# Opening of a fused GFNet and ELU-MLP kernel: x and a half-size table first, the filter straight into SBUF, a plain first unit, and the weights converted late

## The chip, the cores and the metric

The kernel runs on one core of a Trainium2 chip. The metric is the time of one execution in microseconds (us) on the device, as the median of several runs. A profile of one execution gives the rows that are read here. Its engines are TensorE (PE, with its weight loads as PEld), VectorE (DVE), ScalarE (ACT), GpSimd (POOL) and SyncE (SP), and 16 DMA engines that serve the queues of SP, ACT and POOL.

## The reference

```python
X = np.fft.rfft(x, axis=1)                       # x: (8, 3008, 256) float32
Y = X * (filt_r + 1j * filt_i)[None]             # filter: (1505, 256)
y = np.fft.irfft(Y, n=3008, axis=1)
h = y.reshape(24064, 256) @ w_in                 # w_in: (256, 2048) float64
g = np.where(h > 0, h, np.exp(np.minimum(h, 0)) - 1)
out = (g @ w_out).astype(np.float32)             # w_out: (2048, 256) float64
```

A Fourier filter runs along the sequence of each of the eight batches, and a two-layer perceptron with the ELU nonlinearity runs over all 24064 tokens. The weights come as float64, and the kernel works in float32.

## The kernel before

The transform of length 3008 is factored as 47 x 64 and done by matrix products with small tables. Rows of x are paired with their mirror rows: forward rows lie in the lower 64 partitions and mirrored rows in the upper 64. The stages of a batch are: a (the first factor, six units of four rows each), transposes, b (the second factor), the product with the filter on VectorE, bi and n (the inverse factors). The result y goes through a DRAM buffer (`yd`) between bi and n. The n units give tiles of y for the perceptron.

The perceptron is done in units (b, m), six per batch, and each unit in four quads q, one for each quarter of the 2048 hidden columns. One level of Strassen's scheme cuts the eight block products of a quad to seven, for the up projection (`up_steps`, line 607) and for the down projection (`down_steps`, line 692). For this the input needs four differences (`n_sums`, line 584), the weights need four sums (`w_sums`, line 839), and the up products are combined by additions on VectorE (line 630) and copies on ScalarE (line 633). ELU is Relu and Exp on ScalarE (lines 639 and 640) and a maximum on VectorE (line 644). The items (b, m, q) are numbered as quads 0 to 191, 24 to a batch. In the stream of quad i the up products of item i alternate with the down products of item i-1. The transform of batch b+1 is spread over the quads of batch b by a plan, `at(quad, place, fn)`, written by hand: places 2 and 3 lie after the third and fifth step of the first half of the quad, place 0 after that half, place 1 at the end. The order of the instructions on each engine is the order of the program (`manual_schedule`, line 878). Semaphores of DMAs issued by SP and ACT come from eight lanes used in turn, so such a DMA can have to wait for an earlier one of its lane; POOL's DMAs have eight lanes of their own.

The opening (lines 878 to 1007) does batch 0's transform by functions of its own, while nothing else is there to overlap:

- `x_load_first` (293) loads a unit of x in two DMAs, and its table `tf` in a third. `a_first` (303) does 16 matmuls a unit and copies the result to `zt` on ScalarE (315). `t_first` (318) transposes on TensorE.
- `f_arrange` (848) rearranges the filter in DRAM, from the inputs to the buffer `fd`, by DMAs of POOL; `f_read_first` (359) reads it into the tile `ff`. `f_pairs` (867) later rearranges `fd` into the order for the other batches.
- The loop over g from 0 to 9 runs `b_first` (381, with the four VectorE products of lines 376 to 379), `bi_first` (395) and `y_write_first` (407). `y_read` (524) then brings y back, and `n_unit(0, 0)` (line 545, `n_whole`) makes the first input tile.
- The weights are 16 pieces of 128 x 512 float64, two for w_in and two for w_out in each quarter. `w_fetch` (776) loads one as pairs of 32-bit words. `w_split` (801) takes the mantissa and the exponent by two bit operations on VectorE. `w_float` (807) makes floats of them by four operations on ScalarE (814). `w_join` (816) joins sign, mantissa and exponent on VectorE (820, 822, 829 or 835). `step(k)` is the split and float of piece k with the join of piece k-1. In the kernel before, pieces 0 to 6 are converted between the units of a, pieces 7 to 10 inside the g loop, 11 to 13 after it, and 14 and 15 in quads 0 to 2.

PSUM has four banks for general use, handed out in turn by `bank` (197), and four for the down products and the transposes.

Of the kernel before, what the change touches and what calls it, by code (L numbers as in the profile page):

```python
# [11 lines left out]
FP32 = mybir.dt.float32  # L12
# [29 lines left out]
def _make_tables():  # L42
# [27 lines left out]
    tf = np.ascontiguousarray(ta.reshape(P, H, 4, K2).transpose(0, 1, 3, 2)).reshape(P, H, P)  # L70
# [43 lines left out]
    lie = np.concatenate([2 * np.arange(24), 2 * np.arange(24) + 1])  # L114
    gb[:, :, lie] = gb[:, :, :48].copy()
    for t in (gr, gi):
        for o in (0, 64):
            t[o + lie] = t[o:o + 48].copy()
# [3 lines left out]
    tw = np.ascontiguousarray(tn[:, 0:8].reshape(4, K2, 8, 2, 2, 32).transpose(1, 0, 2, 4, 3, 5)).reshape(P, 8, P)  # L122
# [12 lines left out]
def kernel(  # L135
# [47 lines left out]
    edges = glob.tile([P, 2], FP32, name="edges")  # L183
    unit = glob.tile([P, P], FP32, name="unit")
    fd = fdp.tile([NG, 2, 48, 2, 2, D], FP32, name="fd")
# [107 lines left out]
    def x_load_first(c):  # L293
        t = xs[0, c]
        u = 1 if c == 0 else 0
        nc.sync.dma_start(t[HALVES[0]].rearrange("p u d -> p (u d)"), raw(x, XC * c, [[N1 * D, 64], [1, XC * D]]))
        nc.sync.dma_start(t[HALVES[1], u:XC, :], raw(x, N1 - XC * c - u, [[N1 * D, 64], [-D, XC - u], [1, D]]))
        if c < 2:
            nc.sync.dma_start(tas[0, c], tf_d[:, 4 * c:4 * c + 4, :])
        elif c % 2 == 0:  # L300
            nc.sync.dma_start(tas.pop(("pair", c // 2)), tf_d[:, 4 * c:4 * c + 8, :])
# [16 lines left out]
    def t_first(g):  # L318

        t = t2s[0, g] = t4p.tile([P, 4, D], FP32, tag="t4", name="tf") if g % 4 > 1 else t2[:, g % 4]  # L320
        for j in range(2):
            i = j + 2 * (g % 2 if g < 4 else 0)
            ps = psO.tile([P, 2, 256], FP32, tag="po%d" % i, name="po%d" % i)
            for u in range(2):
                k = 4 * g + 2 * j + u
                for dh in range(2):
                    nc.tensor.transpose(ps[0:ROWS, u, ts(dh, P)], zt[k // 16][dh][:, ts(k % 16, ROWS)], eye)  # L327
            nc.scalar.activation(out=t[0:ROWS, 2 * j:2 * j + 2, :], in_=ps[0:ROWS], func=AXT.Copy)
# [30 lines left out]
    def f_read_first(g, t):  # L359
        for a, r in enumerate((LO, HI)):  # L360
            nc.gpsimd.dma_start(t[r].rearrange("p c u d -> p (c u d)"), fd[g, a].rearrange("q c u d -> q (c u d)"))
# [12 lines left out]
    def products(re, im, f, sr, si, p, q):  # L374

        nc.vector.tensor_tensor(out=sr, in0=re, in1=f[:, 0], op=ALU.mult)
        nc.vector.tensor_tensor(out=si, in0=re, in1=f[:, 1], op=ALU.mult)
        nc.vector.scalar_tensor_tensor(out=p, in0=im, scalar=-1.0, in1=f[:, 1], op0=ALU.mult, op1=ALU.mult)
        nc.vector.tensor_tensor(out=q, in0=im, in1=f[:, 0], op=ALU.mult)
# [144 lines left out]
    def y_read(b, m, *parts):  # L524
        t = t4s[b, m] = t4p.tile([P, 4, D], FP32, tag="t4", name="t4")
        for k in parts or (slice(0, K2),):
            if whole(b, m):
                r = slice(4 * k.start, 4 * k.stop)
                nc.sync.dma_start(t[r], yds[b].rearrange("k (p i) d -> (k p) i d", p=4)[r, 4 * m:4 * m + 4, :])
                continue  # L530
            for r in range(2):
                o = 64 * r
                nc.sync.dma_start(t[o + 2 * k.start:o + 2 * k.stop].rearrange("q i d -> q (i d)"),
                                  yds[b][k.start + r:k.stop:2].rearrange("k (p i) d -> k p (i d)", p=4)
                                  [:, :, 4 * m * D:4 * m * D + 4 * D])
# [9 lines left out]
    def n_whole(b, m):  # L545
# [10 lines left out]
        b11, b12, b21, b22 = rows  # L556
        t = yp.tile([P, 2, 256], FP32, tag="yb", name="yb")[:, :, 0:h]
# [42 lines left out]

    COMBO = {1: 0, 2: 2, 3: 6, 4: 3, 5: 4, 6: 5, 7: 1}
# [5 lines left out]
    def up_steps(b, m, q):  # L607

        h = half(m)
# [82 lines left out]
    def down_steps(b, m, q):  # L692
        h = half(m)
# [82 lines left out]
    def w_fetch(k, queue=nc.gpsimd):  # L776
        q, j = divmod(k, 4)

        if k in (3, 4, 14, 15):
            wd = t2[:, k % 11 - 3].rearrange("p u d -> p (u d)")  # L780
        elif k == 10:
            wd = t1p.tile([P, XC, D], FP32, tag="t1", name="wd").rearrange("p u d -> p (u d)")
        elif k in (6, 7, 8, 9):
            wd = xp.tile([P, 2, 2, D], FP32, tag="xc", name="wd").rearrange("p k u d -> p (k u d)")
        else:
            wd = fbufs[{5: 0, 11: 0, 12: 1, 13: 2}.get(k, k)].rearrange("p c u d -> p (c u d)")
# [14 lines left out]
    def w_split(k):  # L801
        m, e, f, l = wts[k] = wtmp[{9: 2, 10: 1, 11: 0, 12: 3, 13: 4, 15: 5}.get(k, k % 2)]
# [4 lines left out]
    def w_float(k, *parts):  # L807
        m, e, f, l = wts[k]
        ef = e.bitcast(FP32)
        steps = ((l, wds[k][:, :, 0], AXT.Identity, 2.0 ** -52, 0.0), (f, m, AXT.Identity, 2.0 ** -20, 1.0),  # L810
                 (ef, e, AXT.Relu, -8.0, edges[:, 0:1]), (e, ef, AXT.Relu, -1.0, edges[:, 1:2]))
        for i in parts or range(4):
# [3 lines left out]
    def w_join(k, parts=(0, 1)):  # L816
        q, j = divmod(k, 4)
        m, e, f, l = wts[k]
        if 0 in parts:
            nc.vector.scalar_tensor_tensor(out=e, in0=wds.pop(k)[:, :, 1], scalar=0x80000000, in1=e,  # L820
                                           op0=ALU.bitwise_and, op1=ALU.bitwise_or)
            nc.vector.tensor_tensor(out=f, in0=f, in1=l, op=ALU.add)
        if 1 not in parts:
            return
        e = e.bitcast(FP32)
# [10 lines left out]
        if j % 2 == 1 and k < 7:  # L836
            w_sums(k)

    def w_sums(k, engine=nc.vector, parts=(0, 1, 2, 3)):
# [4 lines left out]
        for i in parts:  # L844
            o, x, y, op = sums[i]
            engine.tensor_tensor(out=o, in0=x, in1=y, op=op)

    def f_arrange():

        for c, src in enumerate((filt_r, filt_i)):  # L850
            for a in range(2):
                nc.gpsimd.dma_start(fd[:, a, 0:48:2, c, :, :].rearrange("g q u d -> q g (u d)"),
                                    raw(src, 2 * a, [[64 * D, 24], [4 * D, NG], [1, 2 * D]]))
                for u in range(2):
                    g0 = 1 if a == u == 0 else 0
                    for j, n in ((0, 16), (16, 7)):
                        nc.gpsimd.dma_start(fd[g0:NG, a, 1 + 2 * j:2 * (j + n):2, c, u, :].rearrange("g q d -> q g d"),
                                            raw(src, 64 * (j + 1) - 4 * g0 - 2 * a - u,
                                                [[64 * D, n], [-4 * D, NG - g0], [1, D]]))

                g0 = 0 if a else 1
                nc.gpsimd.dma_start(fd[g0:NG, a, 47, c, :, :].rearrange("g u d -> g (u d)"),
                                    raw(src, 4, [[2 * D, NG - g0], [1, 2 * D]]))
            nc.gpsimd.dma_start(fd[0, 0, 1:48:2, c, 0, :], raw(src, 32, [[64 * D, 24], [1, D]]))
            nc.gpsimd.dma_start(fd[0, 0, 47:48, c, 1, :], raw(src, 4, [[D, 1], [1, D]]))

    def f_pairs(c, u):

        src = fd.rearrange("g a q c u d -> (g a) q c u d")[:, :, c, u, :]
        dst = fp.rearrange("g (a u) k c h d -> (g a) u k c h d", u=2)[:, u, :, c, :, :]  # L870
        nc.sync.dma_start(dst[:, :, 0, :], src[:, 0:48:2, :])
        g = 1 - u
        nc.sync.dma_start(dst[g:, 1:24, 1, :], src[g:, 1:46:2, :])
        nc.sync.dma_start(dst[g:, 0, 1, :], nil_d[g:])
        if u == 0:
            nc.sync.dma_start(dst[0, :, 1, :], src[0, 1:48:2, :])

    with tc.manual_schedule():


        with tc.tile_pool(name="boot", bufs=1) as bp:
            ff = bp.tile([P, NG, 2, 2, D], FP32, name="ff")
# [9 lines left out]

            for z in zt[0] + zt[1]:
                nc.gpsimd.memset(z.rearrange("p (k r) -> p k r", r=ROWS)[:, :, 48:64], 0.0)
            for k in (1, 2, 3):
                w_fetch(k)
            f_arrange()
            w_fetch(0, nc.sync)
            for c in range(NXC):
                x_place_first(c)  # L900
            for c in range(3):
                x_load_first(c)
            w_fetch(4, nc.sync)
            nc.scalar.memzero(ff[:, 0:NG // 2])
            nc.vector.memset(ff[:, NG // 2:NG], 0.0)
            def places(m, e, c):
                wtmp.append((m.bitcast(U32), e.bitcast(U32), c[:, 0], c[:, 1]))

            def flat(t):
                return t.rearrange("p a b -> p (a b)")  # L910

            places(*(kp.tile([P, 512], FP32, tag=t, name=n) for t, n in (("k0", "wm"), ("k1", "we"))),
                   kp.tile([P, 2, 512], FP32, tag="c", name="wfl"))
            places(*(flat(sdp.tile([P, 2, D], FP32, tag="sd", name=n)) for n in ("wm", "we")),
                   t1p.tile([P, XC, D], FP32, tag="t1", name="wfl").rearrange("p (a b) d -> p a (b d)", a=2))
            for i, v in enumerate((1151.0 * 2 ** 23, 255.0 * 2 ** 23)):
                nc.vector.memset(edges[:, i:i + 1], v)
# [7 lines left out]
            for k in range(3):  # L925
                step(k)
            w_fetch(5, nc.sync)
            for c in (3, 4):
                x_load_first(c)
            a_first(0)  # L930
            w_fetch(6, nc.sync)
            x_load_first(5)
            nc.sync.dma_start(once, once_d)
            nc.sync.dma_start(gs, gs_d)
            step(3)
            for c in (1, 2):
                a_first(c)
                w_fetch(c + 6, nc.sync)
            step(4)
            a_first(3)  # L940
# [200 lines left out]
```

## Time and profile before

| what | value |
|---|---|
| time, median of 3 runs (lowest to highest) | 2551.03 us (2550.78 to 2551.74) |
| profiled execution: its time | 2553.3 us |
| profiled execution: span, first to last instruction | 2551.5 us |
| PE busy, share of the span | 2517.5 us, 99% |
| DVE busy | 2112.0 us, 83% |
| ACT busy | 1527.3 us, 60% |
| first matmul starts | 13.08 us |
| first product of `b_first` starts | 48.29 us |
| last product of the filter on VectorE ends | 75.15 us |
| first up product of quad 0 starts | 89.14 us |
| quad 6 starts | 164.46 us |

The first rows are read on the profile's page, the last five in its timeline. An engine's share counts matmuls, activations and vector operations; the issue of DMAs is not counted as busy. In the windows, the columns behind the length are busy us and number of instructions for PE, PEld, DVE, ACT and POOL, then the mean clock that TensorE was granted (1.00 is full), the mean busy share of the 16 DMA engines, and what they moved in GB/s. In the chain, a piece is work that the next piece waited for. A line of a matmul counts two records for one instruction of the program.

### The profile page before, as it was taken

The numbers are of one execution on the slowest core, as the hardware profiler recorded it, in microseconds if no ns is written. First come the engines' busy times: TensorE is split into PE (matmuls) and PEld (weight loads), VectorE is DVE, ScalarE is ACT, GpSimd is POOL, SyncE is SP. The second block draws the span as 40 slices with busy tenths as digits, with TensorE's granted clock in tenths as the row PEclk, the third lists the DMA queues.
The fourth block names the chain that finished last, engine by engine and source line by source line (L and its number), as shares of the span: only waits on it lengthen the run. The fifth ranks groups of instructions, "written<-read, shape, count | busy, mean of one in ns | idle before, by whom it ended". The sixth has DMA issues, their size and how long they took to land.

```text
span 2551.5 us, 45225 instructions
## 1 busy us (share of the span) xinstructions
PE 2517.5 (99%) x17266; PEld 2162.0 (85%) x17266; DVE 2112.0 (83%) x3649; ACT 1527.3 (60%) x2680; POOL 159.4 (6%) x315
## 2 busy tenths in 40 slices
PE   6999999999999999999999999999999999999999
PEld 5788889888898888988889888888889888898888
DVE  6878888888788888888888888788897888876766
ACT  6765556655565565565555656555555655555555
POOL 5001000010000000000000000000100010000000
PEclk9999999999999999999999999999999999999999
DMA  9662213422134231433215331243213322120010
GB/s 281 176 183 68 66 36 82 126 68 68 42 99 102 66 70 40 112 87 74 55 40 139 73 80 36 69 125 82 63 41 81 91 61 65 36 46 19 20 28 17
DMA packets 229452, 198.35 MB, mean 78 GB/s; under 512 B 128326, under 2 KB 201558, under 8 KB 229236
## 3 DMA queue, kind: packets, MB, share of 16 engines
q1 hardware_dynamic: 214740, 164.57, 26.2%
q0 software_dynamic: 14000, 30.44, 4.3%
q8 instruction: 136, 2.23, 0.4%
q14 instruction: 80, 0.66, 0.1%
q10 hardware_dynamic: 496, 0.46, 0.1%
HBM read 123.50 MB, written 78.12 MB: 79 GB/s over the span
## 4 chain that ended last, share of the span: by engine, by line
PE 97%; DMA 2%; DVE 1%; SPq 0%; issue 0%; ACT 0%; DVEq 0%
PE po L704 45%; PE phs L622 25%; PE phd L622 13%; PE pha L622 6%; PE psn L574 2%; PE pf L427 1%; PE pv L499 1%; DMA xc<-in_x_dram 1%; PE psa L246 1%; PE po L372 1%; DMA x<-in_x_dram 1%; PE po L327 0%; PE psr L372 0%; PE psa L265 0%; PE psa L308 0%
## 5 line engine op out<-in xcount | busy, mean ns | idle before, releaser
L704 PE MATMUL po<-g,wo 128*128 128x256 f32 (+1 forms) x5376 | 1317.6, 377 | 0.0
L704 PEld LDWEIGHTS po<-g,wo 128*128 128x128 f32 x5376 | 1010.7, 190 | 166.2 <-issue 52.4
L633 ACT ACTIVATE g<-phs 128x512 f32<-128x512 f32 (+1 forms) x576 | 338.8, 588 | 742.9 <-PE phs L622 741.5
L640 ACT ACTIVATE e<-e 128x512 f32<-128x512 f32 (+1 forms) x768 | 477.3, 621 | 24.4
L644 DVE SCALAR_TENSOR_TENSOR g<-e,g 128x512 f32<-128x512 f32 (+1 forms) x576 | 387.4, 673 | 13.6 <-ACT e L640 13.2
L630 DVE TENSOR_TENSOR g<-phd,g 128x512 f32<-128x512 f32 (+1 forms) x384 | 258.9, 674 | 158.1 <-ACT e L640 107.6
L622 PE MATMUL phs<-y,wi 128*128 128x256 f32 (+1 forms) x1536 | 387.6, 375 | 0.0
L622 PE MATMUL phd<-y,wi 128*128 128x256 f32 (+1 forms) x1504 | 380.3, 375 | 0.0
L639 ACT ACTIVATE e<-g 128x512 f32<-128x512 f32 (+1 forms) x576 | 354.4, 615 | 34.2 <-DVE g L630 26.7
L622 PEld LDWEIGHTS phs<-y,wi 128*128 128x128 f32 x1536 | 291.7, 190 | 33.3 <-ACT g L633 0.2
L622 PEld LDWEIGHTS phd<-y,wi 128*128 128x128 f32 x1504 | 284.8, 190 | 35.1 <-DVE g L630 2.7
L644 DVE SCALAR_TENSOR_TENSOR g<-e,phs 128x512 f32<-128x512 f32 (+1 forms) x192 | 129.9, 677 | 115.2 <-ACT e L640 115.2
L622 PE MATMUL phs<-yt,wi 128*128 128x256 f32 (+1 forms) x768 | 193.9, 375 | 0.9 <-ACT g L633 0.9
L622 PE MATMUL phs<-yb,wi 128*128 128x256 f32 (+1 forms) x768 | 193.8, 375 | 0.6 <-ACT g L633 0.6
L622 PE MATMUL pha<-yb,wi 128*128 128x256 f32 (+1 forms) x736 | 185.9, 375 | 0.0
L639 ACT ACTIVATE e<-phs 128x512 f32<-128x512 f32 (+1 forms) x192 | 112.3, 585 | 111.9 <-PE phs L622 111.8
L622 PEld LDWEIGHTS phs<-yt,wi 128*128 128x128 f32 x768 | 145.7, 190 | 17.9 <-ACT g L633 1.4
L622 PEld LDWEIGHTS phs<-yb,wi 128*128 128x128 f32 x768 | 143.9, 190 | 19.3 <-ACT g L633 1.0
L366 POOL DMA_DIRECT2D fall<-fp x224 | 110.1, 499 | 722.1 <-DVE r L472 697.1
L622 PEld LDWEIGHTS pha<-yb,wi 128*128 128x128 f32 x736 | 139.8, 190 | 16.1
L630 DVE TENSOR_TENSOR g<-pha,g 128x512 f32<-128x512 f32 (+1 forms) x192 | 129.3, 673 | 28.3 <-PE pha L622 28.3
L681 DVE TENSOR_TENSOR g<-g,g 128x512 f32<-128x512 f32 (+1 forms) x192 | 130.7, 681 | 6.7
(177 smaller groups left out, 2077.9 us busy)
## 6 DMA issues: line engine op xcount, KB each, us to landing
yd<-t SPq DMA_DIRECT2D x127, 192.0 KB
t<-yd SPq DMA_DIRECT2D x92, 256.0 KB
fall<-fp POOLq DMA_DIRECT2D x224, 96.0 KB, 2.9
t<-z SPq DMA_DIRECT2D x224, 96.0 KB
out_dram<-o SPq DMA_DIRECT2D x624, 32.0 KB
z<-t SPq DMA_DIRECT2D x144, 128.0 KB
xc<-in_x_dram SPq DMA_DIRECT2D x84, 128.0 KB
xc<-in_x_dram SPq DMA_DIRECT2D x161, 64.0 KB
```

Source lines behind the costliest of these rows:

```text
L246: nc.tensor.matmul(ps[k][1][a:a + 32, u, :], w[r, u, 32 * o:32 * o + 32], parts[o][r, u, :], start=True, stop=True, tile_position=(32 * k, a))
L366: nc.gpsimd.dma_start(t[32 * a:32 * a + 24].rearrange("p c u d -> p (c u d)"), fp[g, a].rearrange("q c u d -> q (c u d)"))
L372: nc.tensor.matmul(ps[:, u:u + w, :], table[k, v, :], r[k, u:u + w, :], start=n == 0, stop=n == len(rhs) - 1)
L574: nc.tensor.matmul(o, t[r, i - 4 * m, ds(dh * P + 64 * c, 64)], w[r, i - 4 * m, :], start=True, stop=True)
L622: nc.tensor.matmul(ps[:, a, 0:h], w_in[q][:, COMBO[n], a, :], y[n], start=start and a == 0, stop=True, skip_group_check=True)
L630: nc.vector.tensor_tensor(out=g[o], in0=i0, in1=i1, op=ALU.add)
L633: nc.scalar.activation(out=g[o], in_=i0, func=AXT.Copy)
L639: nc.scalar.activation(out=e, in_=src, func=AXT.Relu, scale=-1.0)
L640: nc.scalar.activation(out=e, in_=e, func=AXT.Exp, scale=-1.0)
L644: nc.vector.scalar_tensor_tensor(out=g[n], in0=es[n], scalar=1.0, in1=src, op0=ALU.subtract, op1=ALU.max)
L681: nc.vector.tensor_tensor(out=b12, in0=b22, in1=b12, op=ALU.subtract)
L704: nc.tensor.matmul(po[i][:, u, 0:h], w_out[q][:, COMBO[n], a, :], g[n][:, a, :], start=q == 0 and a == 0 and n in (1, 3, 6, 4), stop=True, ...
```

## The change

1. The table of the first factor is stored at half size (128 x 24 x 64) and loaded into the space of `t3f`. VectorE makes the full table of each unit from it (`a_table`: one copy and two multiplications by a sign). x is loaded first, ahead of everything but this table; then `once` and `gs`, two small constant tables.
2. The filter is loaded straight into `ff` by `f_first`, with forward rows and mirrored rows in separate ranges of partitions: forward rows on SP's queue ("f", 14 DMAs), the first 16 mirrored rows of a half on ACT's queue behind units 2, 3 and 5 of a ("m", 12 DMAs), the other 7 on POOL's queue ("s", 12 DMAs). `f_arrange`, `f_read_first` and `fd` are gone, and `f_pairs` reads the inputs, by one DMA more each.
3. All weights are fetched on SP behind the filter. `w_float` has three operations instead of four: the scaling of the mantissa has gone into the add of `w_join`, which is now a multiply-add. Pieces 0 and 1 are begun at the last two rounds of the g loop, 2 to 8 follow before `n_unit(0, 0)`, and 8 to 15 are finished in quads 0 to 3. All eight `w_sums` are done on VectorE in quads 3 to 6.
4. The first unit (0, 0) is done plainly, by eight block products (`plain_ups`, `plain_downs`), without `n_sums`, sums of weights and additions.
5. The writes of y go by POOL's queue (the last one's second half by ACT's), and the read of y for unit (0, 0) too. The units of x and a of batch 1, with their z writes, come one quad later (quads 3, 3, 4, 4, 5, 5 instead of 2, 2, 3, 3, 4, 4); `n_unit(0, 1)` is at place 0 of quad 2.

```diff
     def x_load_first(c):
...
-        if c < 2:
-            nc.sync.dma_start(tas[0, c], tf_d[:, 4 * c:4 * c + 4, :])
-        elif c % 2 == 0:
-            nc.sync.dma_start(tas.pop(("pair", c // 2)), tf_d[:, 4 * c:4 * c + 8, :])
+    def a_table(c):
+        t = th[:, XC * c:XC * c + XC]
+        o = tas[0, c].rearrange("p u (k f) -> p u k f", f=4)
+        nc.vector.tensor_copy(out=o[:, :, :, 0:4:2], in_=t)
+        for f, k in ((1, 1), (3, 0)):
+            nc.vector.tensor_scalar(out=o[:, :, :, f], in0=t[:, :, :, k], scalar1=signs, scalar2=None, op0=ALU.mult)
...
+    def f_first(k, n, parts, queue):
+        for c, src in enumerate((filt_r, filt_i)):
+            for a in range(2):
+                o, row, e = 64 * a, 16 * a + k, 1 if k == a == 0 else 0
+                if "f" in parts:
+                    queue.dma_start(ff[o:o + 24, c, k:k + n].rearrange("q k d -> q (k d)"),
+                                    raw(src, row, [[64 * D, 24], [1, n * D]]))
+                for j, m, part in ((0, 16, "m"), (16, 7, "s")):
+                    if part in parts:
+                        queue.dma_start(ff[o + 24 + j:o + 24 + j + m, c, k + e:k + n],
+                                        raw(src, 64 * (j + 1) - row - e, [[64 * D, m], [-D, n - e], [1, D]]))
+            if k == 0 and "f" in parts:
+                queue.dma_start(ff[24:48, c, 0], raw(src, 32, [[64 * D, 24], [1, D]]))
...
+    def plain_ups(b, m, q):
...
+        def step(i, j, k):
+            if k == 0:
+                held[i, j] = bank("php")
+            n, ps = held[i, j]
+            for a in range(2):
+                nc.tensor.matmul(ps[:, a, 0:h], w_in[q][:, 2 * k + i, a, :], rows[k][j],
+                                 start=k == a == 0, stop=True, skip_group_check=True)
+            if k == 1:
...
+                nc.scalar.activation(out=e, in_=src, func=AXT.Relu, scale=-1.0)
+                nc.scalar.activation(out=e, in_=e, func=AXT.Exp, scale=-1.0)
+                nc.vector.scalar_tensor_tensor(out=g[i, j], in0=e, scalar=1.0, in1=src, op0=ALU.subtract, op1=ALU.max)
...
     def w_join(k, parts="ab"):
...
+            w_sign(k)
+            nc.vector.scalar_tensor_tensor(out=f, in0=m, scalar=2.0 ** -20, in1=l, op0=ALU.mult, op1=ALU.add)
...
     with tc.manual_schedule():
...
+            nc.sync.dma_start(flat_th[:, 0:2 * XC], tf_d[:, 0:2 * XC])
+            for c in range(NXC):
+                x_load_first(c)
+                if c == 0:
+                    nc.sync.dma_start(flat_th[:, 2 * XC:H], tf_d[:, 2 * XC:H])
+            nc.sync.dma_start(once, once_d)
+            nc.sync.dma_start(gs, gs_d)
+            parts = ((0, 4), (4, 4), (8, 8))
...
+            for c in range(2):
+                a_table(c)
+            nc.vector.memset(ff[:, 1], 0.0)
+            for c in range(2, NXC):
+                a_table(c)
+            for c in range(NXC):
+                a_first(c)
+                if c == 0:
+                    for k, n in parts:
+                        f_first(k, n, "s", nc.gpsimd)
+                        f_first(k, n, "f", nc.sync)
+                if c in (2, 3, 5):
+                    f_first(*parts[c // 2 - (c == 2)], "m", nc.scalar)
             tn_read(0, 0)
+            for k in range(8):
+                w_fetch(k)
             for g in range(4):
                 t_first(g)
             for g in range(NG + 2):
...
                 if g >= 2:
-                    y_write_first(g - 2, (nc.sync, nc.scalar if g == NG + 1 else nc.sync))
+                    y_write_first(g - 2, (nc.gpsimd, nc.scalar if g == NG + 1 else nc.gpsimd))
+                if g >= NG:
+                    step(g - NG)
...
+            for k in range(8, 10):
+                w_fetch(k)
+            step(2)
+            for k in range(10, 16):
+                w_fetch(k)
+            for k in range(3, 8):
+                step(k)
+            w_split(8)
+            w_float(8)
+            w_join(7)
             warm = psO.tile([P, 512], FP32, tag="po2", name="warm")
...
         n_unit(0, 0)
-        n_sums(0, 0)
...
+        line = [part for k in range(9, 17) for part in ((k, "s"), (k - 1, "a"), (k - 1, "b")) if part[0] < 16]
+        for quad, *counts in ((0, 0, 0, 2, 0), (1, 2, 2, 2, 2), (2, 2, 2, 2, 2), (3, 2, 2, 0, 1)):
+            for place, n in zip((2, 3, 0, 1), counts):
+                at(quad, place, convert, n)
+        for quad, place, fn, k in ((3, 0, w_sums, 1), (3, 1, w_sums, 3), (4, 2, w_sums, 5), (4, 1, w_sums, 9), (5, 2, w_sums, 7),
+                                   (5, 1, w_sums, 13), (6, 2, w_sums, 11), (6, 0, w_sums, 15)):
+            at(quad, place, fn, k)
```

In the diff, `convert(n)` takes the next n parts of `line`: the split and float of a piece ("s"), the sign and multiply-add of its join ("a"), or its final multiplication ("b").

## Prediction

> **What bounds the kernel now.** First the page's busy shares and its chain, then one table of windows, then TensorE's waits and the opening's chain. The busy line and the windows (columns: stretch, length, then busy us and instructions of each engine, granted clock, DMA share, GB/s):
>
> ```profile
> PE 2517.5 (99%) x17266; PEld 2162.0 (85%) x17266; DVE 2112.0 (83%) x3649; ACT 1527.3 (60%) x2680; POOL 159.4 (6%) x315
> ```
> ```profile
> 0.00:20.00 20.00, 5.25 (x23) 5.02 (x24) 13.99 (x26) 16.18 (x22) 12.52 (x27) 1.00 0.93 268
> 20.00:40.00 20.00, 12.47 (x59) 11.48 (x58) 9.81 (x21) 11.59 (x26) 8.01 (x14) 0.87 1.06 334
> 50.00:78.00 28.00, 28.00 (x222) 14.53 (x221) 25.30 (x46) 21.06 (x38) 7.06 (x12) 1.00 0.84 225
> 89.00:165.00 76.00, 72.18 (x489) 64.32 (x489) 62.35 (x117) 52.99 (x94) 4.51 (x9) 1.00 0.63 180
> 165.00:2551.00 2386.00, 2381.67 (x16387) 2052.93 (x16385) 1986.25 (x3410) 1409.98 (x2472) 121.40 (x242) 1.00 0.28 67
> ```
> After 165 us TensorE is 99.8% busy, and the change leaves that code alone. So the time is decided by when quad 6 begins (164.46 here): each us by which it moves moves the end. Before 40 us the DMA engines are full (0.93, 1.06) and TensorE is mostly idle. The chain says for what (start, us, what):
>
> ```profile
> 3.20 10.88 DMA xc<-in_x_dram
> 14.09 13.14 DMA xc<-in_x_dram
> 27.25 12.84 DMA x<-in_x_dram
> 40.22 3.77 PE psa L308 x16
> ...
> 78.12 2.66 DMA yd<-t
> 80.86 3.68 DMA t<-yd
> 84.55 1.26 issue
> 85.80 3.56 PE psn L552 x16
> ```
> x waits behind weights and the filter's rearrangement; then come the transform, the trip of y through DRAM, and n_unit. The up products of quad 0 start at 89.14. Between them and quad 6 TensorE's only named waits are short ones:
>
> ```profile
> PE phd L622 <- DVE g L630: 2.3, 2, 1.7
> PE phs L622 <- ACT g L633: 1.5, 2, 0.9
> ```
>
> **Part 1, x first: gain 19.4 us at b_first(0).** After the change half the tables and x (3.86 MB together) are all that is queued ahead. The first 20 us move 268 GB/s (first window), 290 between 5 and 10; at 0.29 MB/us x0 is there at 5.3 us, x5 at 16.1. a_first takes 3.75 us on a half clock (rows at 13.08 to 40.22), six of them. If TensorE warms, one is 1.95 (an estimate, the warm n_unit's 16 records). The copies out of c=2 are done at 13.6. Here a new wait comes in: a DMA of SP or ACT waits for an earlier one in its semaphore lane, over both queues. gs on SP waits for ACT's first mirrored filter load, which is issued after c=2's copies (lands about 16.9, 2.7 to 3.7 us as for y); the fourth mirrored load waits for gs (20.0); behind it on ACT stand the copies of c=4 and c=5 (22.8), behind these more loads, and behind those the first transposed copy (26.4), for which b_first(0) waits. By this it starts at 28.9, against 48.29. Bounds: 27 if no load holds ACT up; 34 if all six a_first run at 3.75 (5.3+22.5, transposes 3.8, one copy) and a load lands 2 us late. The 18 table operations on VectorE (0.4 to 0.7 each) are done by 13 us, beside the loads, also with the 3.47 us memset among them. The filter's 3.1 MB, no longer written to DRAM and read back, and weights 0 to 7 (4.2 MB) follow x at the same rate and land by 42 us. Nothing needs the weights before 54, so this is hidden by 12 us; without that cover it would cost what it overruns.
>
> **Part 2, the transform loop: 25.5 us.** From b_first(0) to the last products it took 26.9 (48.29 to 75.15), of which 1.58 was ScalarE waiting for a yd write. y is now written by POOL and conversions are out of the loop; I take 25.5. The last products end at P = 54.4 (before 75.15), 20.8 us earlier.
>
> **Part 3, conversions now stand alone ahead of quad 0: cost 10.** Before, six steps lay under the x loads. After, nine splits and eight joins are ahead of ScalarE's y copy or beside it. Their rows (behind the first bar: busy us and mean ns of one):
>
> ```profile
> L804 DVE TENSOR_SCALAR wm<-wd 128x512 uint32<-128x512 uint32 x4 | 1.7, 423 | 5.4 <-DMA wd<-in_moe_w_out_dram 5.4
> L820 DVE SCALAR_TENSOR_TENSOR we<-wd,we 128x512 uint32<-128x512 uint32 x5 | 3.4, 684 | 0.0
> L829 DVE TENSOR_TENSOR wi<-wfl,we 128x512 f32<-128x512 f32 x6 | 4.2, 692 | 0.2
> L814 ACT ACTIVATE we<-we,edges 128x512 f32<-128x512 uint32 (+1 forms) x26 | 18.7, 720 | 0.9 <-DVE zq L805 0.5
> ```
> Start to start, a split is 0.33+0.34, a join 0.60+0.72+0.61 = 1.93, taken as 1.95 (the new multiply-add priced like L822's add), a float on ScalarE 0.57+1.38. Joins bind: 2.62 a step. join(1) ends at P+8.35 (splits, two floats and the last t copies ahead of it), join(6) five steps later at P+21.45, split(8) at P+22.1; float(8)'s two exponent operations 1.4, y0's copy 0.55: up products may start at P+24.1 = 78.5. The y trip and n_unit (2.7+3.7+3.6 after the last copies) are done about P+14, hidden by some 10 us. So quad 0 starts 10.6 us earlier than 89.14, not 20.8.
>
> **Part 4, plain first unit: cost 6.05.** 16+16 matmuls a quad for 14+14, four quads: 16 more by 0.378 (two records of 0.35 to 0.38 each, start to start 0.189). It drops n_sums (four operations of 0.41) from the path and the adds and subs of L630 and L680 to L684 from VectorE, which frees the room for the late conversions.
>
> **Part 5, stalls until quad 6: 10 for 6.0.** Before, 89.14 to 164.46 is 75.3 us, of which the matmuls fill 69.3. For after I walked the order of the three engines by the rows above and 1.2 us of ScalarE and 0.6 of VectorE a block (Relu, Exp; max). It gives: a cold start, since TensorE has idled some 10 us, 1.5 to 1.9 (n_unit 3.56 cold, 1.95 warm); in quad 2 block 3 waits 2.8 for a bank, as n_unit(0,1) holds two and the max of block 1 stands behind float(13) on ScalarE; in quad 3 block 0 waits 4.3 for w_join(13), behind the maxes of quad 2; a_unit in quad 3 waits 2.2 for maxes behind w_sums and x_unit; quad 5 0.8; b_unit after quad 6 about 1.4, since z is now written one quad later (before: z writes issued 153.75, reads issued until 164.76, a 12 us trip for 14 us of work after a_unit ends its copies). Sum 13.1. Ends: 5 (only the cold start and half the rest) and 15. I take 10, nearer the walk, as 7.1 of it in two places ends with VectorE free for 2 to 4 us just before and so falls with any earlier arrival.
>
> The page "TensorE: Matmul & The Clock Gate" of the Trainium skill (Part 1) says the array starts at half clock, needs about 3.4 us of activity, and falls back after an idle window; by that the cold start would cost 1.7, as my rows have it, and 13.1 would stand. The window 20 to 40 agrees (0.87 with gaps of 1 to 3 us), though the 1.00 shown where a_first still took 3.75 does not.
>
> **Other moves, at nothing.** POOL now issues the y writes (14 by 0.5 us, and it is otherwise idle then); if its landing is slower than SP's by even 8 us, conversions still cover it. SP takes over the weight loads (0.33 to 0.8 each) and, for f_pairs, one more load in each of quads 1 to 4 (0.6); it has 10 us of room a quad before b_unit wants anything. The eight w_sums (1.68 each) go into quads 3 to 6 on VectorE, w_sums(7) among them, which POOL did; they are in the walk.
>
> **Sum.** -10.6 (start of quad 0) +6.05 (plain) +4.0 (stalls) = -0.55: quad 6 at about 163.9. The profiled execution has span 2551.5 and time 2553.3, 2.3 above the median of 2551.03; taken from the median the forecast is 2550.5. About 0.2% (5.1 us) is what a measurement of this kernel can tell from no change.
>
> **Rivals.** *Faster:* the walk's two bank and weight waits are mostly hidden (VectorE's gaps), stalls 5 to 6, and b_first(0) at 27.5: -12 +6.05 -0.5 = -6.5, 2544.5 (2540 to 2546). For it: only 3.8 us of named waits in 76 us before, with as much conversion work inside. Against: ScalarE is given 7 floats of 1.95 and 16 blocks of 1.2 in some 40 us. Chance 0.34.
>
> *Slower:* the opening's coupled lanes. If filter loads hold ScalarE's queue so that b_first(0) comes at 36, quad 0 starts at 85.6: -3.5 +6.05 +5 (stalls 11) = +7.5, 2558.5. It decides from 34.6 (5.1+0.55 later than 28.9) for slower by over 0.2%. For it: small loads took up to 6.8 us under full DMA (ff<-fd, 192 KB); against: only x and table are ahead, and the queue thins after 16 us. Chance 0.18. The page "DMA: Bandwidth & Descriptors" of the Trainium skill (on why a semaphore counts 16) says a transfer uses the largest number of engines up to 16 that divides its slowest dimension: 12 for 24 rows, 7 for 7. By it the 1.6 MB of forward rows would need 7.2 us in place of 5.4, which by itself moves b_first(0) by under 2 and leaves the forecast. No trace shown so far has such loads.
>
> *It does not do what it says:* the loads of x stay slow (0.2 MB/us with 1 KB pieces of mirrored rows), x5 at 22 and cold a_firsts, b_first(0) at 34.5 and the loop unchanged: +6.5, 2557.5. Chance 0.04.
>
> **Numbers.** Forecast, within 0.2%: 0.44, 2546 to 2556. Faster 0.34, slower 0.22. The range for 8 in 10 is 2541 to 2559: it reaches into both sides until about one tenth is left out at each.
>
> **What would show it.** Opening right: first t copy near 26, first psr near 29, last products near 54. Part 3: no TensorE work but warm matmuls and n_unit between 57 and 78, and y0's copy straight behind an L894 activation. If y0's copy comes at 70, conversions are cheaper than the rows say and I am too slow by 8. Part 5: waits of php on VectorE in quads 2 and 3 of 2 to 4 us; if none is over 1, the faster case holds. Wrong altogether: quad 6 to the end other than 2387 us, since then something after quad 6 has moved.

## The result and the profile after

The changed kernel takes 2574.72 us (median of 4 runs, 2574.35 to 2577.3) against 2551.39 of the kernel before (2550.78 to 2552.41): ratio 1.0093, 95% interval 1.0076 to 1.0111. It is slower by 23.3 us, where 2550.5 was forecast. The profiled execution has a span of 2575.5 and a time of 2577.3, so the spans differ by 24.0, and these are taken apart here.

The busy shares and the windows of the profile after (columns as in the prediction):

```profile
PE 2533.5 (98%) x17298; PEld 2173.7 (84%) x17298; DVE 2097.1 (81%) x3634; ACT 1512.6 (59%) x2652; POOL 145.6 (6%) x289
```
```profile
0.00:20.00 20.00, 12.54 (x66) 12.16 (x67) 7.61 (x24) 8.85 (x14) 8.27 (x20) 1.00 0.94 207
20.00:40.00 20.00, 12.82 (x74) 11.12 (x74) 0.00 (x0) 7.87 (x20) 0.00 (x0) 0.70 0.82 141
...
120.00:140.00 20.00, 13.96 (x64) 12.93 (x63) 11.89 (x24) 12.14 (x20) 0.00 (x0) 0.91 0.01 2
...
190.00:2575.00 2385.00, 2377.18 (x16355) 2048.05 (x16353) 1979.53 (x3397) 1407.70 (x2468) 122.26 (x242) 1.00 0.27 67
```
TensorE does get work earlier (12.54 us in the first 20, against 5.25), but between 20 and 40 us VectorE has nothing at all to do, and the DMA engines, busy for 0.82, move only 141 GB/s. A second hole is at 120 to 140: TensorE is idle for 6 us while the DMA engines rest too, so it waits for VectorE or ScalarE. And the last window is no longer full: 7.8 us are idle, where before it was 4.3.

The chain of the opening (start, us, what):

```profile
11.43 6.75 PE psa L307 x32
18.72 6.18 DMA ff<-in_filt_r_dram
25.28 3.01 DMA ff<-in_filt_r_dram
29.67 3.95 DMA ff<-in_filt_r_dram
33.64 1.09 ACTq L367
...
35.43 3.66 PE po L325 x16
```
In place of the x loads, three loads of the filter stand on the chain, and they stand there by ScalarE's queue (ACTq). ScalarE's own timeline says what was behind them (start, us, engine, line, count, idle before and what ended it):

```profile
18.72 0.43 ACTq L367 DMA_DIRECT2D ff<-in_filt_r_dram  x1
...
24.92 0.80 ACTq L367 DMA_DIRECT2D ff<-in_filt_r_dram  x2
25.76 2.50 ACTq L367 DMA_DIRECT2D ff<-in_filt_i_dram  x2
28.30 0.38 ACT L314 ACTIVATE zt<-psa 128x256 f32<-128x256 f32 x1 [6.93 <-DMA ff<-in_filt_r_dram]
...
34.78 2.06 ACT L326 ACTIVATE t<-po 112x512 f32<-112x512 f32 x4 [4.16 <-DMA ff<-in_filt_r_dram]
```
The copies of unit 4 of a wait 6.93 us, and the transposed copies 4.16, for filter loads that these copies do not read. They wait since they are queued behind them. x was late as well: the matmuls of unit 5 of a start at 24.10, after a wait for x, where the prediction had x5 there at 16.1.

```profile
24.10 3.48 PE L307 MATMUL psa<-t,x 128*128 128x128 f32 x16 [2.36 <-DMA x<-in_x_dram]
```
TensorE's waits from 0 to 220 us (total, times, longest):

```profile
PE psa L307 <- DMA xc<-in_x_dram: 7.5, 2, 5.3
PE php L634 <- ACT y L564: 3.9, 1, 3.9
PE php L634 <- DVE wi L916: 3.6, 1, 3.6
PE psn L563 <- issue: 3.5, 1, 3.5
PE psn L588 <- DMA t<-yd: 3.2, 2, 2.2
PE warm L1044 <- DVE wi L916: 3.1, 1, 3.1
PE php L634 <- DVE g L641: 2.4, 1, 2.4
...
PE phd L697 <- DVE g L705: 2.0, 1, 2.0
```
The waits of 3.6 and 2.4 us for VectorE (`wi`, `g L641`) are two waits of the walk: join 13 in quad 3, and a bank in quad 2. The wait for y (`t<-yd`) is new: unit (0, 3) waits for its y in quad 8, where the forecast had nothing.

Four marks split the 24.0: the last filter product P, the first up product of quad 0, the first matmul of b_unit behind quad 6 (`pf`), and the end.

| stretch, us | before | after | difference | forecast |
|---|---|---|---|---|
| start to P | 75.15 | 66.71 | -8.4 | -20.8 |
| P to the first up product | 13.99 | 24.64 | +10.6 | +10.2 |
| first up product to pf | 87.50 | 103.36 | +15.9 | +10.05 |
| pf to the end | 2374.9 | 2380.8 | +5.9 | 0 |

### The profile page after: what moved, and what is told of

It is laid out like the page before. It is cut to its first block, busy times and chain, and to the rows that moved or that the text cites. A ratio compares the mean times of both kernels' runs of the same rounds, so it can differ in the third digit from the quotient of the medians.

```text
span 2575.5 us, 45261 instructions
## 1 busy us (share of the span) xinstructions
PE 2533.5 (98%) x17298; PEld 2173.7 (84%) x17298; DVE 2097.1 (81%) x3634; ACT 1512.6 (59%) x2652; POOL 145.6 (6%) x289
## 4 chain that ended last, share of the span: by engine, by line
PE 94%; DMA 2%; ACT 1%; DVE 1%; SPq 1%; issue 0%; ACTq 0%; POOL 0%; DVEq 0%
PE po L781 44%; PE phs L697 24%; PE phd L697 12%; PE pha L697 6%; PE psn L588 2%; PE pf L437 1%; PE pv L509 1%; PE psa L241 1%; DMA xc<-in_x_dram 1%; DMA ff<-in_filt_r_dram 1%; PE po L657 0%; DMA yd<-t 0%; DMA ta<-ta_t 0%; PE po L325 0%; PE psa L307 0%
## 5 line engine op out<-in xcount | busy, mean ns | idle before, releaser
L781 PE MATMUL po<-g,wo 128*128 128x256 f32 (+1 forms) x5264 | 1294.6, 378 | 0.0
L781 PEld LDWEIGHTS po<-g,wo 128*128 128x128 f32 x5264 | 990.4, 190 | 165.9 <-issue 51.7
L708 ACT ACTIVATE g<-phs 128x512 f32<-128x512 f32 (+1 forms) x564 | 332.3, 589 | 739.5 <-PE phs L697 738.2
L715 ACT ACTIVATE e<-e 128x512 f32<-128x512 f32 (+1 forms) x752 | 468.0, 622 | 23.9
L719 DVE SCALAR_TENSOR_TENSOR g<-e,g 128x512 f32<-128x512 f32 (+1 forms) x564 | 380.1, 674 | 13.2 <-ACT e L715 12.9
L697 PE MATMUL phs<-y,wi 128*128 128x256 f32 (+1 forms) x1504 | 380.0, 375 | 0.0
L714 ACT ACTIVATE e<-g 128x512 f32<-128x512 f32 (+1 forms) x564 | 347.5, 616 | 33.5 <-DVE g L705 26.6
L697 PEld LDWEIGHTS phs<-y,wi 128*128 128x128 f32 x1504 | 285.6, 190 | 33.0
L697 PEld LDWEIGHTS pha<-yb,wi 128*128 128x128 f32 x736 | 139.8, 190 | 16.1
```

Of the source, the lines that this page charges most:

```text
L697: nc.tensor.matmul(ps[:, a, 0:h], w_in[q][:, COMBO[n], a, :], y[n], start=start and a == 0, stop=True, skip_group_check=True)
L708: nc.scalar.activation(out=g[o], in_=i0, func=AXT.Copy)
L714: nc.scalar.activation(out=e, in_=src, func=AXT.Relu, scale=-1.0)
L715: nc.scalar.activation(out=e, in_=e, func=AXT.Exp, scale=-1.0)
L719: nc.vector.scalar_tensor_tensor(out=g[n], in0=es[n], scalar=1.0, in1=src, op0=ALU.subtract, op1=ALU.max)
L781: nc.tensor.matmul(po[i][:, u, 0:h], w_out[q][:, COMBO[n], a, :], g[n][:, a, :], start=q == 0 and a == 0 and n in (1, 3, 6, 4), stop=True, ...
```

## The experiments

Each was timed against the kernel before on the same chip (2551.3 to 2551.9 us). The theory after reading the trace: four separate things, namely ScalarE's loads in the opening, the conversions, their remainder in the quads, and the units of batch 1 that were moved by a quad. The rival: the filter's loads themselves are slow, and everything behind P is the plain unit.

### The long mirrored loads on another queue

```diff
-                        f_first(k, n, "s", nc.gpsimd)
+                        f_first(k, n, "ms", nc.gpsimd)      # e1_m_sp: "s" here, "fm" by nc.sync
...
-                if c in (2, 3, 5):
-                    f_first(*parts[c // 2 - (c == 2)], "m", nc.scalar)
```


> The 16-row mirrored filter loads go to POOL's queue, beside the 7-row ones, in place of ScalarE's. Theory (lanes): the changed kernel's b_first starts at 39 instead of 29 us because ScalarE's copies stand behind its own loads, which wait 6.2, 3.0 and 4.0 us for loads of the shared lanes; then the first psr comes at 29 to 32 and the time is 2565 to 2567, 8 to 10 below the changed kernel's 2574.7. Rival (the loads themselves): the 24-, 16- and 7-row loads are slow (141 GB/s at a DMA share of 0.82 between 20 and 40 us), so the products on VectorE wait for the filter instead, the last product still ends at 64 to 67, and the time stays within 3 of 2574.7.

> The same loads go to SP's queue, each behind the forward load of its half. Lanes: ScalarE is as free as with POOL, so the same 2565 to 2567, if SP's 26 loads with eight in flight are in time; their issue alone would be 26 by some 0.5 to 1.5 us, 13 to 39 us, so part 0 is there by 32 and part 2 by 50. Rival (the loads themselves): within 3 of 2574.7; if SP's queue becomes the hold, weights come late as well and it is slower than 2575.

Measured: 2570.66 us by POOL (ratio 1.0067, 1.0050 to 1.0084) and 2570.63 by SP (1.0070, 1.0055 to 1.0085). The start of b_first in e1_m_sp, in TensorE's timeline:

```profile
28.95 0.43 PE L381 MATMUL psr<-t,once 48*64 48x256 f32 x1
```
It is at 28.95 (30.97 by POOL), 10.1 earlier than in the changed kernel and where the forecast had it (28.9). VectorE's first product waits for TensorE in e1_m_sp, and P comes at 55.51 (57.53 by POOL). So the queue was the cause of the late b_first, and not the loads' own slowness. But the time falls by only 4.1, and the 8 to 10 of the theory are missed. The first up product comes 7.0 earlier, at 84.31, not 11: ScalarE's copies now wait for writes of y in this kernel, while the DMA engines are full (busy for 1.02 at 366 GB/s between 40 and 60 us, when the weights load):

```profile
47.61 0.60 ACT L414 ACTIVATE t<-po 128x512 f32<-128x512 f32 x1 [3.99 <-DMA yd<-t]
...
55.32 0.60 ACT L414 ACTIVATE t<-po 128x512 f32<-128x512 f32 x1 [4.54 <-DMA yd<-t]
```

### Batch 1's units back in their quads

```diff
-                for c, s in enumerate((3, 3, 4, 4, 5, 5) if b == 1 else (0, 0, 3, 3, 4, 4)):
+                for c, s in enumerate((2, 2, 3, 3, 4, 4) if b == 1 else (0, 0, 3, 3, 4, 4)):
```


> The changed kernel with batch 1's units of x and a back in quads 2, 2, 3, 3, 4, 4. Theory: 6.0 us are lost after quad 6 (2393.1 us from there to the end, 2387.0 before) because z is written and read one quad later, and with it SP's stores and the read of y for unit (0, 3), for which TensorE waits 3.2 us; then that part returns to 2387 to 2388 and the time is 2568 to 2570, less what four vector operations more in quad 2 cost, 0 to 3. Rival: the read of y is late because it is four DMAs in place of two; then 2574, and the wait in quad 8 stays.

Measured: 2567.77 us (1.0057, 1.0042 to 1.0072), 7.0 less than the changed kernel, and 8.9 less in span. From pf to the end it is 2375.2 again (before 2374.9), and TensorE's wait for y is gone, though y is still read by four DMAs in place of two; the rival falls. The stretch before pf shrinks too, from 103.4 to 100.0. In the changed kernel SP's timeline shows how the trip of z pushes the read of y:

```profile
189.25 3.18 SPq L355 DMA_DIRECT2D t<-z  x8
...
200.72 11.18 SPq L831 DMA_DIRECT2D out_dram<-o  x24
211.94 0.42 SPq L532 DMA_DIRECT2D tn<-tn_t  x1
212.41 2.85 SPq L544 DMA_DIRECT2D t<-yd  x4
```
The reads of z wait for z to land and hold SP; then come loads of x, then 24 stores of 0.47 us each, and only after these the read of y, for which unit (0, 3) is waiting at 216. Moved back by a quad, the reads of z start at 171.65 and the read of y at 200.70.

### The plain unit alone, on the kernel before

```diff
+        if plain(b, m):
+            return plain_ups(b, m, q)        # and plain_downs
...
-        n_sums(0, 0)
...
-        if j % 2 == 1 and k < 7:
-            w_sums(k)                        # all w_sums to quads 3 to 6
```


> The kernel before with only the first unit done plainly, and the sums of the weights moved to quads 3 to 6 as in the changed kernel. By the matmuls it costs 16 instructions of 0.378 = 6.05; it takes away n_sums(0, 0) (1.6 us, on the path to quad 0's third product) and the stalls of quads 0 to 2 on additions (3.2 us). So 2551.4 + 6.05 - 2 to 4.8 = 2553 to 2555.5. Rival: with one bank a block it stalls more than Strassen does, then 2558 to 2562, and the plain unit alone would explain the changed kernel's stalls.

Measured: 2557.31 us (1.0021, 1.0012 to 1.0031), 5.4 more than before, so both theories miss it. The sums of the weights are moved along with the unit. Its first up product comes 0.4 earlier (88.76), and from there to pf it takes 92.1 us in place of 87.5. So the plain unit costs 4.6 in that stretch, where its matmuls alone are 6.05; what it takes away is worth 1.4, less than the 2 to 4.8 expected. The time lies just short of the rival's 2558 to 2562, and still it explains less than a third of the changed kernel's 15.9.

### The writes of y on SP

```diff
-                    y_write_first(g - 2, (nc.gpsimd, nc.scalar if g == NG + 1 else nc.gpsimd))
+                    y_write_first(g - 2, (nc.sync, nc.scalar if g == NG + 1 else nc.sync))
```


> e1_m_sp (2570.6) with the writes of y on SP's queue, as in the kernel before, in place of POOL's. In e1_m_sp the first up product comes 28.8 us after the last product, 4 more than in the changed kernel, and ScalarE's bi copies wait 3.99, 1.01, 4.54 and 1.57 us for earlier writes of y. Theory (POOL's queue is the slow one): these waits go, conversions start at once, 2565 to 2567. Rival (the DMA engines are full of weights, whichever queue asks): 2569 to 2572, with the same waits.

Measured: 2577.88 us (1.0104, 1.0089 to 1.0119), 7.3 more than e1_m_sp: both theories were wrong. ScalarE's timeline in this kernel:

```profile
54.54 0.60 ACT L414 ACTIVATE t<-po 128x512 f32<-128x512 f32 x1 [12.88 <-DMA yd<-t]
```
The writes of y stand behind the loads of pieces 0 to 7 on SP's queue. The first yd issue there is at 47.63, though b_first had begun two us earlier than in e1_m_sp. With the weights on SP, the change was right to take the writes of y off it.

### Conversions into the transform loop

```diff
+                        if k == 0:
+                            for j in range(3):
+                                w_fetch(j)
...
+                if g < 3:
+                    step(g)
                 if g >= NG:
-                    step(g - NG)
+                    step(g - NG + 3)
```


> e1_m_sp with weights 0 to 2 fetched behind the first part of the filter, and steps 0 to 2 of the conversion done in rounds 0 to 2 of the transform loop; steps 3 to 8 stay behind it. Theory (conversions set the start of quad 0, 2.62 a step): three steps less are 7.9, the loop grows by 2 to 3, so 2565 to 2567. Rival (the read of y sets it): quad 0 starts within 2 of 84.3, and the time within 2 of 2570.6, or higher, since the filter comes later.

Measured: 2565.02 us (1.0056, 1.0039 to 1.0072), 5.6 less than e1_m_sp and just inside the theory's range, but not by its path. P moves from 55.51 to 57.49, as expected. But the first up product comes at 82.37, only 1.9 earlier and not 6, for now n_unit is the late one: it starts at 78.83, and no conversion is left in front of it. Of the 6.9 in span, 1.9 lie ahead of quad 0, 3.1 between there and pf, where quad 0 starts warm (the first 40 matmul records take 7.92 us in place of 9.41), and 1.9 behind pf.

### Conversions left out, to see what lies behind them

```diff
-            for k in range(3, 8):
-                step(k)
+            w_join(2)
             w_split(8)
             w_float(8)
-            w_join(7)
```


> The changed kernel with the conversion of pieces 3 to 7 left out (these weights stay zero; all loads stay). Theory (conversions set the start of quad 0): five steps by 2.62 less, quad 0 starts at 78 to 79 in place of 91.35, and the time is 2562. Rival (the trip of y is nearly as late: n_unit's matmuls ended at 87.4 in the changed kernel): quad 0 starts at 87 to 88.5 and the time is 2571 to 2572.

Measured: 2565.34 us (1.0056, 1.0041 to 1.0071). TensorE's timeline:

```profile
78.78 3.43 PE L563 MATMUL psn<-tn,t 128*128 128x128 f32 x16 [2.34 <-issue]
82.00 8.01 PE L634 MATMUL php<-y,wi 128*128 128x224 f32 x40
```
P comes 5.3 earlier here (61.44), which is no work of the conversions, as they stand behind P: x is there earlier, and the matmuls of unit 5 of a start at 20.58 in place of 24.10. With the same loads of x, this start lies anywhere between 20.9 and 24.9 in the profiles of the other kernels, and POOL's memset of the zero weights puts most of its filter loads later here; which of the two it was is not shown. So the time says little, and the stretch behind P counts. From P to the first up product it is 20.6 us in place of 24.6: 13 us of conversions taken away are worth 4.0. The trip of y with n_unit is the second chain, at P+20.6, not at P+14. In the changed kernel too the matmuls of n_unit end at 87.4, which is P+20.7.

### All four edits together

The kernel has the edits of e1_m_sp, e2_units_early, e4_y_sp and e5_conv_loop.

> All four edits on the changed kernel: all of the filter's long loads on SP, writes of y on SP, steps 0 to 2 in the loop, batch 1's units in quads 2, 2, 3, 3, 4, 4. If the causes add: 2574.7 - 4.1 - 7.0 - 4.5 - 4.5 = 2554.6, still 3 above the kernel before. If the start of quad 0 is held by the trip of y, the edits for conversions give nothing: 2559 to 2563.

Measured: 2562.50 us (1.0044, 1.0029 to 1.0059), in the second range. n_unit waits 7.3 us for y; the writes of y on SP, unknown to be harmful when it was put together, are in it.

### The last weights behind the read of y, and more steps in the loop

```diff
-                w_fetch(k)                  # pieces 8 to 15, behind y_read(0, 0)
+                w_fetch(k, nc.gpsimd)
...
-                if g < 3:                   # e9_more_loop only
-                    step(g)
+                if g < 3 or g in (5, 6):
+                    step(g if g < 3 else g - 2)
```


> e5_conv_loop (2565.0) with batch 1's units back in quads 2 to 4, and pieces 8 to 15 of the weights fetched by POOL behind the read of y instead of by SP beside the writes of y. The units are worth 7 to 9 (e2_units_early). In e5_conv_loop n_unit starts 22 us after the last product, and POOL waits 5.5 us for the last write of y to land while SP moves these pieces. Theory (the trip of y now sets the start of quad 0 and the weights beside it make it long): n_unit comes 4 to 7 earlier, so 2551 to 2554. Rival (conversions of pieces 3 to 8 are still the longer chain): 2556 to 2558, with ScalarE's y copy straight behind a conversion.

> e8_fetch_late with steps 3 and 4 also inside the transform loop, in rounds 5 and 6. If conversions set the start of quad 0 after e8: 3 to 5 below e8_fetch_late. If the trip of y does: the loop, full on VectorE from round 4 on, grows by 2.6 a step, so the last product and everything behind it comes up to 5 later than in e8_fetch_late.

Measured: e8_fetch_late (with the units of e2_units_early and the loop of e5_conv_loop) 2557.41 us (1.0021, 1.0011 to 1.0030), e9_more_loop 2558.95 (1.0028, 1.0016 to 1.0040). The theory's 2551 to 2554 is missed, and the time of e8_fetch_late is in the rival's range. n_unit starts at 75.54, 3.3 earlier than in e5_conv_loop (78.83), just short of the theory's 4 to 7. But now ScalarE waits for piece 8, which has become late, and y's copy stands straight behind a conversion, as the rival had it:

```profile
77.92 0.69 ACT L894 ACTIVATE wd<-wd 128x512 f32<-128x512 uint32 x1 [3.46 <-DMA wd<-in_moe_w_in_dram]
78.72 1.48 ACT L894 ACTIVATE we<-we,edges 128x512 f32<-128x512 uint32 x2
80.10 0.96 ACT L564 ACTIVATE y<-psn 128x448 f32<-128x448 f32 x2
```
So the first up product comes only 1.7 earlier, at 80.68. P is at 61.34, 3.9 later than in e5_conv_loop with the same loop, though the loop starts 1.0 earlier. VectorE waits 3.14 us for a load of the filter, up to 49.12, against 1.35 in e5_conv_loop; TensorE then waits for VectorE, its granted clock is 0.50 between 52 and 56 (1.00 in e5_conv_loop), and VectorE waits another 2.7 for TensorE, which it does not in e5_conv_loop. Two more steps in the loop put P at 63.53 and n_unit at 79.16: no gain. That is the rival's side, but not a clean test, as ScalarE waits 8.75 us for piece 8 there. Neither kernel beats the kernel before.

### Conversions in the quads left out

```diff
-            for place, n in zip((2, 3, 0, 1), counts):
-                at(quad, place, convert, n)
+            pass
```


> e2_units_early (2567.8) with the conversions inside quads 0 to 3 left out: the joins of pieces 8 to 15 and the splits and floats of 9 to 15 (those weights are zero, set by POOL before quad 0; all loads stay). From the first up product to the first pf it is 87.5 us in the kernel before, 92.1 with the plain unit alone, 100.0 in e2_units_early. Theory (the late conversions cost the 7.9 between): 92 to 93, and the time is 2560 to 2561. Rival (cold clock and one bank a block cost it): 97 or more, and the time is 2565 or more.

Measured: 2564.13 us (1.0043, 1.0026 to 1.0059). Its start is later (first up product at 95.36), so only the stretch counts: 95.3 us to pf, between the two theories. By pieces, from the first up product to the first matmul of the a units in quads 2, 3 and 4, and on to pf:

| kernel | to a in quad 2 | to a in quad 3 | to a in quad 4 | to pf | sum |
|---|---|---|---|---|---|
| e3_before_plain | 32.3 | 14.7 | 14.7 | 30.4 | 92.1 |
| e10_no_quad_conv | 34.05 | 14.7 | 14.7 | 31.8 | 95.3 |
| e2_units_early | 36.6 | 16.4 | 16.6 | 30.4 | 100.0 |

Without the late conversions quads 2 to 4 run as fast as with early ones. They cost 2.55 + 1.7 + 1.9 = 6.1 there. By the sums it is only 4.7, since e10_no_quad_conv takes 1.4 more in the last column, in front of pf; the cause of that is open. The 1.75 that e10_no_quad_conv still has over e3_before_plain in the first column is the cold start: the first 40 matmul records of quad 0 take 9.63 us after 13.9 us of idleness, and 7.87 in e3_before_plain, where n_unit ran just before. The page "TensorE: Matmul & The Clock Gate" of the Trainium skill (Part 1) states a half clock until some 3.4 us of activity have passed; half of that, 1.7, is an estimate for a cold start, and the 1.76 here agrees.

## Why the prediction was wrong, point by point

Against the forecast the span is 24.6 us longer (24.0 in place of -0.55): 10.1 in part 1, 2.2 in part 2, 0.5 in part 3, 5.7 in parts 4 and 5, and 6.1 from the start of quad 6 to the end, where nothing was forecast.

- **Part 1 failed**: b_first(0) came at 39.02, not 28.9. Two terms were too small. x was priced at 0.29 MB/us and moved slower: the first 20 us carried 207 GB/s in all, POOL's 7-row loads ran beside x from 6.0 us on, and the copies of unit 2 ended at 18.9, not 13.6, which is 5.3 of the 10.1. Then the loads on ScalarE's queue held its copies, as the mechanism said, but through ScalarE's own loads and not through gs: the first load on the chain held it for 6.0 us behind the copies of unit 2 (the load took 6.18 in itself), where 3.3 was taken from writes and reads of y; that is 2.7 more. The other two loads, 3.01 and 3.95, were near the price; the remaining 2.1 came between the first load and b_first. A nearer row was at hand, the 6.8 of `ff<-fd`, which the "slower" rival named (as "up to", though it is the median). Without loads on ScalarE's queue b_first comes at 28.95 with an x that is late too (e1_m_sp), so the queue carried most of it. The rival priced this at 36 and 2558.5; the low rate of x was the condition of the rival with chance 0.04. Neither gives the 24, as both have little or nothing behind quad 0.
- **Part 2** held in size: 27.7 from b_first to P, for 25.5. The wait for a write of y, which POOL was to take away, is still there: ScalarE waits 2.50 us for one before 66.02.
- **Part 3** was right in its sum, 24.64 for 24.1, with y's copy straight behind a conversion, as it said:

```profile
89.39 1.48 ACT L894 ACTIVATE we<-we,edges 128x512 f32<-128x512 uint32 x2 [0.64 <-DVE we L884]
90.77 0.96 ACT L564 ACTIVATE y<-psn 128x448 f32<-128x448 f32 x2
```

Wrong was the cover beside it: the trip of y and n_unit, "hidden by some 10 us", ended at P+20.6 (e6_skip), hidden by 4. From the last copy to n_unit's start it took 11.5 us there, where the rows of 2.66 and 3.68 had been taken. Those are from a stretch in which the DMA engines moved 209 GB/s (77 to 85 us before), against 285 in e6_skip (67 to 79); that this load is the reason is argued.
- **Part 4** held in size: 6.05 for the matmuls; the unit alone costs 4.6 in its stretch and 5.4 in time (e3_before_plain).
- **Part 5 failed**: it took 10 for stalls and set aside its own walk of 13.1. To the start of quad 6 it is 91.1 us, which is 15.7 of stalls. The argument for taking less, that waits which end beside an idle engine shrink with earlier arrival, had no row behind it. Its lower end of 5 does not follow from its own terms either: the cold start and half of the other 11.4 are 7.4. Two waits of the walk were there, 2.4 for 2.8 and 3.6 for 4.3. The runs put the late conversions at 4.7 to 6.1 and the cold start at 1.75.
- **"Other moves, at nothing" failed**: units one quad later cost 3.4 before pf and 5.6 after it (e2_units_early), 7.0 in time. The 10 us of room a quad that it gave SP did not count the 24 stores, 11 us of issue, and the reads of z that wait ahead of them. So it was wrong too that the change leaves the code behind 165 us alone.

Put together, by stretches: -8.4 at P, +10.6 for conversions ahead of quad 0, +4.6 plain unit, +7.9 late conversions and cold start, +3.4 and +5.6 for the units, 0.3 open: 24.0. The parts are from executions of different kernels, and the sum can be off by 1 or 2. What stays open is why x moved so slowly, and how much of the filter's slow landing is its piece size and how much its number of rows. No version tried is faster than the kernel before.

## What to carry to other kernels

A DMA issued from an engine that also computes stands in that engine's queue: where it waits for a semaphore lane, every copy behind it waits too (6.93 and 4.16 us here). Put loads of no urgency on a queue that computes nothing, and look at what then stands behind them there (12.88 us for a write of y in e4_y_sp). Work moved out of a stage that is bound by loads was free there and cost 10.6 us in its new place; taking 13 us of it out again gave only 4.0, since a second chain ended just behind. Before moving work, walk the second-longest chain of the new place, with rows taken under the same load. When a step is moved by one round, list everything behind it on the queue that issues its DMAs, stores too: z was moved in quads 3 to 5, and the wait came in quad 8, at a read of y that does not depend on z.

## What the runs showed of the hardware that was not expected

While the filter's loads ran, in ranges of 24, 16 and 7 rows, the DMA engines were busy for 0.82 of the time and moved 141 GB/s (20 to 40 us); while the weights' loads of 128 rows of 2 or 4 KB ran, they moved 376 to 405 GB/s at 1.02 to 1.05 (44 to 56 us) in the same execution. So the busy share does not tell the rate.

TensorE paid again after idle stretches: the first 40 matmul records of quad 0 took 10.15 us in the changed kernel (3.94 us idle before), 9.41 in e1_m_sp (7.23) and 9.63 in e10_no_quad_conv (13.86), against 7.87 to 7.92 where n_unit ran just before them. A short pause is enough where TensorE had not warmed up: in e8_fetch_late n_unit ran for 3.75 us at a granted clock of 0.50, 1.39 us of idleness followed, and the clock stayed at 0.50 up to about 84 us, so that the 40 records took 9.57. In the middle of quad 2 of the changed kernel, after a long warm stretch, a wait of 2.43 us cost little beyond itself: the next 4 records took 1.02 in place of 0.92.
